# Filler matmuls on zeros spread over the first stages of an attention and expert kernel on one core

## The chip, the cores and the metric

The kernel runs on one core of a Trainium2 chip. Its time is device microseconds (us) of one execution, and kernels are compared by the median of their runs. TensorE (PE) multiplies, VectorE (DVE), ScalarE (ACT) and GpSimd (POOL) work element by element, and SyncE (SP) issues transfers. [...]

## What is computed

Two stages, cut from the reference to what matters:

```python
# q, k, v: (2, 8, 576, 64)
q_d, k_d, v_d = (t.reshape(B, H, 144, 4, D).mean(axis=3) for t in (q, k, v))
out_d = softmax(scale * q_d @ k_d.T) @ v_d               # pooled attention
out_up = np.repeat(out_d, 4, axis=2)
mask = np.abs(pos[:, None] - pos[None, :]) < 4           # a narrow band
out_local = softmax(np.where(mask, scale * q @ k.T, -1e9)) @ v
attn_out = out_up + out_local
x = attn_out.transpose(0, 2, 1, 3).reshape(1152, 512)
p = domain_probs / (domain_probs.sum(-1, keepdims=True) + 1e-9)
for e in range(4):                                       # w1: (4, 512, 1024), w2: (4, 1024, 512)
    out += p[:, e:e + 1] * (np.maximum(x @ w1[e], 0) @ w2[e])
```

## The kernel before

The attention is done in four parts, a0 to a3: two batches, each in two halves of 288 positions. The names of steps and tiles follow from that.

- Keys and queries come in with positions on the partitions and are transposed by PE through the identity: k00t, k01t (batch 0, halves 0 and 1), k10t, k11t for keys and a0.qt for queries, each in four steps (`transposed`, L309). A copy (k01te, a0.qte) brings each result out of PSUM.
- Pooled keys and queries are sums over four positions, k01ds and a0.qds on DVE or GpSimd (L342, L343), transposed by k01dt and a0.qdt (`pooled_rows`, L348).
- Pooled attention runs in four groups of two heads. In group 0 of a0: a0.ds0 scores (`dscores`, L628), a0.dm0 and a0.dn0 maxima, a0.de0 exponentials, a0.da0, a0.db0 and a0.dq0 normalisation, a0.dt0 transposes (`dtrans`, L680), a0.dv0 values (`dvalues`, L697).
- Local attention runs in three tiles of queries: a0.sc1.0 and a0.sc1.1 are two halves of the scores of tile 1 (`scores`, L485; for a0 a matmul with the mask goes ahead, L475), then max, sub, exp, sum and norm, block transposes on DVE (a0.blk) and a0.pv1 the values (`values`, L565).
- a0.xs, a0.xh and a0.xl add both attentions and split the sum into xhi and xlo, the experts' input in two parts.

The experts follow. Expert 0 takes the tokens in four chunks, m00 to m03, and forms its products in three terms each from halves of the weights (whi, wlo) and of x. m00.m0 to m00.m7 are the first products of chunk 0 (`m1`, L730: twelve matmuls of 128x256, into a tile m00h each). ACT's m00.r0 takes the positive part (`relu`, L737), and DVE's m00.l0 takes the rest (`rest`, L741); m00h has been read then. m00.o00 and on are the second products (L755). The other chunks and experts 1 to 3 come after 90 us and fill the rest of the span.

The order of all this is written out by hand. Each piece of work is a named step, `steps` holds them, and `ORDER` (L22) is the list in which the loop at L1043 runs them; what a step issues is put at the end of its engine's instructions. Waits come from the data: an instruction waits until what it reads is written, and until the buffer that it writes into is free. The buffers matter here. PSUM tiles come from three pools (L145 to L147): ps_s, ps_g with three buffers, ps_m with three buffers. A tile takes the next buffer of its pool in turn, and the buffer passes on only when the last instruction that uses its former tile is done. ps_m serves two tiles of scores of a0 (a0sb), all m00h tiles, the second products, and the tile of the fillers:

```python
WARM = [14, 0, 0, 0, 0, 0, 0, 0, 0, 0, 0, 0, 0, 1, ...]      # L21
wz = big.tile([P, 64], F32, name="wz")                        # L177
def warm(i, n):
    if "wps" not in T:
        T["wps"] = ps_m.tile([P, 512], F32, tag="m", name="wps")
    for _ in range(n):
        nc.tensor.matmul(T["wps"][:64, :64], wz, wz, start=True, stop=True)
for i, n in enumerate(WARM):
    step(f"warm{i}", "P", [], lambda i=i, n=n: warm(i, n))
```

A filler is one matmul of zeros with zeros, whose result nobody reads. `WARM` says how many each of the 40 steps warm0 to warm39 issues: 31 in all, 22 of them ahead of PE's first real step a0.qdt. The last ones stand ahead of a0.dv1.

Of the kernel before, what the change touches and what calls it, by code (L numbers as in the profile page):

```python
# [21 lines left out]
ORDER = """  # L22
    q0n.0 q0n.1 k00n.0 k00n.1 a0.qds.0 kstart0 q0r.0 k00r.0 q0r.1 a0.qds.1 k00ds.1 k00r.1 warm15 warm36 warm33 warm5
    warm6 warm21 warm37 warm20 warm0 warm22 warm13 warm18 a0.qdt k00t.0 warm10 k00t.1 warm29 a0.qt.0 a0.qt.2 warm34
    warm2 a0.qt.3 a0.qt.1 warm16 k01n.0 v00n.1 v00n.0 k01n.1 v01n.1 warm23 raw100 v01n.0 a1q.1 a1q.2 a1q.0 a1q.3
    vw01 raw101 k00ds.0 a0.qde k01ds.1 v00d.0 a0.start v01d.1 v00d.1 v01d.0 k00te.1 k00te.0 a0.qte.0 warm4 k00t.2
    warm19 a0.qte.2 a0.qte.1 k00t.3 k00te.3 k00te.2 a0.qte.3 a0.sc0.0 a0.sc0.1 warm12 warm25 warm31 warm14 warm30
    k00dt vw00 k01r.1 k01ds.0 warm24 k01dt a0.sc1.0 a0.sc1.1 warm17 k01de k00de k01r.0 a0.max0 a0.sub0 k01t.1 warm11
    k01t.0 a0.max1 k01te.1 a0.sub1 a0.ds1 warm3 a0.ds0 k01t.2 a0.dm1 a0.dn1 k01te.0 a0.exp0 warm39 a0.sc2.0 a0.ds2
    warm7 k01t.3 warm1 a0.exp1 a0.dm0 a0.de1 a0.dn0 a0.sum1 a0.de0 a0.da1 k01te.2 a0.da0 a0.db0 a0.sum0 a0.db1  # L30
    a0.ds3 a0.dm2 a0.dn2 a0.dm3 k01te.3 warm9 a0.sc2.1 warm35 warm38 a0.dq0 a0.dt0 a0.dc0 a0.eps0 a0.dq1 a0.dn3
    a0.rec0 a0.max2 a0.de2 a0.sub2 warm28 warm27 a0.dt1 a0.norm0 a0.da2 a0.dc1 a0.db2 a0.dq2 a0.de3 a0.da3 a0.eps1
    a0.db3 a0.blk0.1 a0.rec1 a0.exp2 a0.blk0.0 a0.sum2 a0.dq3 a0.norm1 whi100.1 wlo100.1 a0.eps2 a0.blk1.1 a0.rec2
    a0.blk1.0 warm26 a0.dv1 a0.dt2 a0.dc2 a0.norm2 whi101.0 a0.dv0 a0.dt3 a0.dv2 warm8 a0.dc3 a0.pv0 a0.dv3 a1.qt.1
    whi100.0 a0.xd a0.xs0 a1.qt.3 a0.pv1 a1.qt.2 a0.blk2.0 a0.blk2.1 vw02 k10r.3 raw200 k10r.2 praw raw201 k10r.1
    a0.xh0 a0.xs1 a0.xl0 wlo100.0 a1.start a1.qte.1 a1.qte.3 wlo101.0 a1.qte.2 a0.pv2 a0.xs2 a0.xh2 a1.qt.0 whi200.1
    whi101.1 wlo101.1 whi200.0 a1.qte.0 a0.xh1 a0.xl2 a1.qd.1 a0.xl1 a1.qd.0 a1.sc1.1 a1.sc2.1 a1.sc2.0 warm32
    a1.sc0.1 m00.m0 a1.ds0 a1.ds1 m00.m3 a1.dm0 a1.dn0 a1.de0 a1.madd2 a1.dm1 a1.da0 wlo200.1 a1.dn1 a1.sc0.0 a1.ds2
    wlo200.0 m00.r0 m00.l0 a1.madd0 whi201.1 a1.de1 whi201.0 m00.r3 a1.db0 a1.dq0 a1.da1 a1.max2 a1.dm2 m00.m2
    a1.sc1.0 a1.dt0 a1.db1 a1.dn2 a1.madd1 a1.dc0 a1.de2 a1.da2 a1.ds3 kstart1 a1.dq1 m00.m1 m00.r2 m00.r1 a1.max0  # L40
    m00.l3 a1.dm3 a1.dn3 a1.db2 wlo201.1 m00.l1 a1.sub0 a1.dq2 a1.sub2 a1.dt1 m00.m6 a1.de3 a1.dc1 m00.m4 m00.r4
    a1.exp0 a1.exp2 k11r.3 vw03 k11r.0 k10r.0 v11n.1 vw05 vw04 v10n.1 k11r.1 k11r.2 a1.da3 a1.dv1 a1.db3 a1.max1
    a1.dq3 m00.l2 a1.dt2 k10t.2 a1.dv0 m00.o00 a1.dt3 a1.dc2 a1.dc3 m00.r6 k10te.2 a1.sum2 a1.sum0 m00.l4 wlo201.0
    a1.eps0 a1.sub1 m00.m5 a1.dv3 k10t.0 a1.dv2 k10t.1 m00.o01 m00.m7 a1.eps2 gate a1.rec2 a1.rec0 a1.norm0 m00.l6
    a1.blk0.0 a1.norm2 a1.exp1 k10te.0 m00.r5 m00.l5 a1.sum1 a1.eps1 k10te.1 a1.xd a1.blk0.1 k11t.1 a1.pv0 k11te.1
    a1.rec1 a1.norm1 m00.r7 a1.xs0 a1.blk2.1 m00.l7 a1.blk2.0 a1.blk1.1 k10t.3 k11t.0 m00.o10 m00.o02 k11t.3 k11t.2
    k11te.0 k10te.3 a1.blk1.0 a1.pv2 k11te.3 k11te.2 k11d.1 a1.pv1 a1.xs1 a1.xh1 a1.xl1 a1.xs2 a1.xh2 a1.xh0
    a2.start a1.xl0 a1.xl2 k10d.0 k10d.1 m00.o11 m00.o03 m00.g0 a2q.3 a2q.2 a2q.1 a2q.0 m00.o12 a2.qt.2 a2.qt.0
    a2.qt.1 m01.m0 a2.qte.1 a2.qte.0 m01.r0 a2.qd.0 k11d.0 m01.m1 v11d.1 a2.qte.2 a2.qt.3 a2.qte.3 a2.qd.1 a2.ds0
    m00.o13 a2.sc0.1 a2.sc0.0 m00.g1 m01.l0 a2.ds2 m01.m3 a2.dm2 a2.dn2 v11n.0 v10n.0 a2.de2 a2.madd0 a2.dm0 a2.dn0  # L50
    a2.de0 a2.da0 a2.da2 a2.max0 a2.db0 m01.r3 m01.r1 a2.dq0 v10d.1 v10d.0 a2.ds1 m01.m2 m01.r2 a2.db2 m01.l1 a2.dq2
    m01.l2 a2.dm1 a2.dn1 a2.sc2.1 a2.sc2.0 a2.sc1.0 a2.dt0 a2.sc1.1 a2.ds3 a2.dt2 a2.dc0 a2.madd1 a2.de1 a2.da1
    a2.max1 m01.l3 a2.madd2 a2.sub1 vw12 a3q.2 v11d.0 vw10 a3q.1 a3q.3 vw11 a3q.0 m01.m6 m01.m4 m01.r4 a2.dc2
    a2.max2 a2.db1 a2.exp1 m01.l4 a2.dm3 a2.dn3 a2.sub2 a2.exp2 a2.de3 m01.m5 m01.r5 m01.o10 a3.qt.1 a2.sum1 a2.dq1
    a2.da3 m01.l5 m01.r6 a2.db3 a3.start a2.dv0 a2.dt1 a2.dv2 m01.o00 m01.m7 a2.dq3 a2.dc1 a2.dt3 m01.o11 m01.l6
    a2.sub0 a2.exp0 a2.dc3 a2.sum0 a2.eps1 a2.rec1 a2.norm1 a2.eps0 a3.qte.1 a2.rec0 a2.norm0 a2.blk1.0 m01.o12
    a2.dv1 a3.qt.0 a3.qt.2 m01.o01 a2.dv3 m01.r7 a2.sum2 a2.blk0.0 a2.eps2 a2.rec2 a2.blk1.1 a2.norm2 a3.qte.2 a2.xd
    a3.qte.0 a2.blk0.1 a2.pv0 a2.blk2.1 a2.blk2.0 a2.pv1 a3.qt.3 m01.o02 vw14 vw13 vw15 a2.pv2 a3.qte.3 a3.sc1.0
    m01.l7 a3.qd.0 a2.xs1 a2.xh1 a2.xs0 a2.xh0 a3.qd.1 a2.xl0 a2.xl1 a3.ds0 m01.o13 m01.o03 a3.sc1.1 a3.sc0.1 m01.g0
# [1011 lines left out]
```

## Time and profile before

| | |
|---|---|
| median of three runs | 482.71 us |
| the runs | 481.98, 482.71, 1521.41 us |
| the profiled execution's own time | 481.98 us |
| its span in the trace | 480.2 us |
| busy: PE, DVE, ACT, POOL | 466.3, 277.8, 162.7, 54.7 us |

The span runs from the first to the last instruction of the profiled execution; 1.8 us of its own time lie around it. One of the three runs is far off the two others, and the median leaves it aside. [...] A busy engine is one that has an instruction under way, at whatever clock.

### The profile page before, as it was taken

Reading aid. Unit: us, or ns where it says so; the run is one execution under the profiler, and the core shown is the slowest. Engines: PE = TensorE matmul, PEld = TensorE weight load, DVE = VectorE, ACT = ScalarE, POOL = GpSimd, SP = SyncE. Lnnn points to the kernel's source line nnn. Section 1 sums busy time; section 2 is a strip of 40 time slices with the busy share of each in tenths; the row PEclk is TensorE's granted clock in tenths of the full one; section 3 lists DMA queues with packets and bytes.
Section 4 is the critical chain, followed back from the end, with each engine's and each line's share of the span. In section 5 each row is a group of like instructions: output and inputs, shape, how many; then the busy total and the mean of one; then the engine's idle time right before and its main releaser. Section 6 shows DMA issues by size and latency. Waiting matters only on the chain.

```text
span 480.2 us, 8723 instructions
## 1 busy us (share of the span) xinstructions
PE 466.3 (97%) x3710; PEld 414.9 (86%) x3710; DVE 277.8 (58%) x493; ACT 162.7 (34%) x277; POOL 54.7 (11%) x68
## 2 busy tenths in 40 slices
...
PEclk8555979999999999999999999999999999999999
...
GB/s 177 210 227 140 60 66 74 129 69 0 68 3 5 41 46 44 89 87 71 105 44 0 1 27 62 46 87 89 44 1 0 60 30 45 45 0 45 44 67 44
DMA packets 49574, 29.90 MB, mean 62 GB/s; under 512 B 26816, under 2 KB 43392, under 8 KB 49536
## 3 DMA queue, kind: packets, MB, share of 16 engines
...
q8 instruction: 29, 0.48, 0.4%
q14 instruction: 9, 0.07, 0.0%
HBM read 26.99 MB, written 2.36 MB: 61 GB/s over the span
## 4 chain that ended last, share of the span: by engine, by line
PE 89%; DVE 5%; DMA 3%; SPq 1%; issue 1%; ACT 1%; ACTq 0%
PE X L936 16%; PE Z L936 8%; PE Y L936 4%; PE m03h L730 3%; PE m03o L755 3%; DMA k01n<-in_k_dram 2%; PE m02h L730 2%; PE m01o L755 2%; PE m01h L730 2%; PE m02o L755 2%; PE m00o L755 2%; PE m00h L730 2%; DVE ptb L556 1%; PE o L993 1%; PE o28None L993 1%; PE o18None L993 1%
## 5 line engine op out<-in xcount | busy, mean ns | idle before, releaser
L975 ACT ACTIVATE hh<-H 128x1024 fp32r<-128x1024 f32 (+1 forms) x30 | 28.9, 974 | 92.1 <-PE o10None L993 4.9
L978 DVE SCALAR_TENSOR_TENSOR ho<-H,hh 128x1024 fp32r<-128x1024 f32 (+1 forms) x30 | 33.6, 1119 | 24.5 <-ACT hh L975 24.5
L888 DVE TENSOR_TENSOR wo<-r,wh 128x1792 fp32r<-128x1792 f32 x12 | 24.3, 2023 | 22.8 <-PE Z L936 18.9
L945 ACT ACTIVATE H<-X 128x576 f32<-128x576 f32 x24 | 15.6, 650 | 55.5 <-PE X L936 55.5
L936 PE MATMUL X<-xc,wh 128*128 128x288 f32 x192 | 33.2, 295 | 0.0
L936 PEld LDWEIGHTS X<-xc,wh 128*128 128x128 f32 x192 | 28.2, 188 | 0.0
L936 PE MATMUL X<-xhi,wo 128*128 128x288 f32 x96 | 20.7, 296 | 0.0
L936 PE MATMUL X<-xlo,wh 128*128 128x288 f32 x96 | 20.6, 296 | 0.0
L936 PE MATMUL X<-xhi,wh 128*128 128x288 f32 x96 | 20.6, 295 | 0.0
L936 PE MATMUL X<-xc,wo 128*128 128x288 f32 x96 | 20.5, 295 | 0.0
L170 ACT CAST wh<-r 128x1792 fp32r<-128x1792 f32 x12 | 20.3, 1689 | 0.3 <-DVE r L880 0.3
L170 ACT CAST v<-q 128x1024 fp32r<-128x1024 f32 x12 | 12.2, 1044 | 15.7 <-PE o18None L993 7.2
L274 POOL TENSOR_TENSOR wlo<-raw,whi 128x1024 fp32r<-128x1024 f32 x7 | 16.7, 2392 | 5.2 <-ACT whi L170 5.1
L949 DVE TENSOR_TENSOR H<-H,Z 128x576 f32<-128x576 f32 x12 | 9.0, 749 | 14.2 <-PE Z L936 14.2
L936 PE MATMUL Z<-xc,wh 128*128 128x288 f32 x96 | 16.6, 294 | 0.0
L936 PEld LDWEIGHTS X<-xhi,wo 128*128 128x128 f32 x96 | 15.6, 188 | 0.2
L936 PEld LDWEIGHTS X<-xlo,wh 128*128 128x128 f32 x96 | 15.4, 188 | 0.0
L936 PEld LDWEIGHTS X<-xhi,wh 128*128 128x128 f32 x96 | 15.4, 188 | 0.0
L936 PEld LDWEIGHTS X<-xc,wo 128*128 128x128 f32 x96 | 15.3, 188 | 0.0
L949 DVE TENSOR_TENSOR H<-H,Y 128x576 f32<-128x576 f32 x12 | 9.0, 749 | 10.8 <-PE Y L936 6.6
L911 DVE TENSOR_TENSOR v<-q,v 128x1024 fp32r<-128x1024 f32 x12 | 14.6, 1219 | 0.9 <-ACT v L170 0.9
L755 PE MATMUL m03o<-whi,m03t 128*128 128x512 f32 x48 | 15.0, 390 | 0.0
...
## 6 DMA issues: line engine op xcount, KB each, us to landing
...
```

What stands on the lines that cost most here:

```text
L170: nc.scalar.copy(out_, in_)
L274: engine(f"wlo{nm}.{i}").tensor_tensor(dst, T["raw" + nm][:, sl], T["whi" + nm][:, sl], ALU.subtract)
L730: nc.tensor.matmul(ps[:, :n], w[:, d, cc:cc + P], x[:, d, n0:n0 + n], start=i == 0, stop=i == len(terms) - 1,)
L755: nc.tensor.matmul(ps[:, cs], T[f"{nm}t{f}"][:, hpart, cc:cc + P], w[:, f % 4, cs], start=f == 0 and x == 0, stop=f == KF - 1 and x == 2,)
L888: engine(f"wo{e}{i}").tensor_tensor(w, T[f"r{e}{i}"], f32(T[f"wh{e}{i}"]), ALU.subtract)
L911: engine(f"vo{e}{q}").tensor_tensor(w[:, 1], T[f"q{e}{q}"], f32(w[:, 0]), ALU.subtract)
L936: nc.tensor.matmul(ps[:, n, :NH // 2], w[:, d * P:(d + 1) * P], x[:, d, n * (NH // 2):(n + 1) * (NH // 2)], start=u == 0 and first_, stop= ...
L945: nc.scalar.mul(dst, at("Z" if c == "t22" else "X"), -1.0)
L949: nc.vector.tensor_tensor(dst, dst, at({"h11": "Y", "h12": "Z", "h22": "X"}[c]), ALU.add)
L975: nc.scalar.activation(htile("hh", t, u), hrows(t, u), AF.Relu)
L978: nc.vector.scalar_tensor_tensor(htile("ho", t, u), hrows(t, u), 0.0, f32(htile("hh", t, u)), ALU.max, ALU.subtract)
L993: nc.tensor.matmul(T[o][:, cs], T[f"{hpart}{e}{t}"][:, f % 4 * 2 + f // 4], T[f"v{e}{q}"][:, w, f % 2 * 512 + cs.start:f % 2 * 512 + cs.stop],
```

## The change

`WARM` gets 42 more entries, 179 fillers in all, and `ORDER` gets the steps warm40 to warm81, each directly in front of a step of PE. Nothing else changes; lines below the two tables move down by three (L206 becomes L209, L730 becomes L733).

```diff
-WARM = [14, 0, 0, ..., 2, 0, 1, 3, 0, 0]
+WARM = [14, 0, 0, ..., 2, 0, 1, 3, 0, 0, 26, 8, 11, 3, 3, 3, 3, 3, 3, 4, 6, 2, 4, 3, 3, 3, ..., 3, 3, 3, 10, 4, 8]
...
-    warm6 warm21 warm37 warm20 warm0 warm22 warm13 warm18 a0.qdt k00t.0 warm10 k00t.1 warm29 a0.qt.0 a0.qt.2 warm34
+    warm6 warm21 warm37 warm20 warm0 warm22 warm13 warm18 warm40 a0.qdt warm41 k00t.0 warm10 k00t.1 warm29 warm42
```

| new steps | fillers | where |
|---|---|---|
| warm40, 41, 42 | 26, 8, 11 | ahead of a0.qdt, k00t.0, a0.qt.0 |
| warm43 to 50 | 28 | from a0.qt.2 to k01dt |
| warm51 to 62 | 36 | from a0.sc1.0 to a0.sc2.1 |
| warm63 to 74 | 36 | from a0.dt0 to a0.pv1 |
| warm75 to 78 | 12 | from a1.qt.2 to a1.sc1.1 |
| warm79, 80, 81 | 10, 4, 8 | ahead of a1.sc1.0 (just behind m00.m2), a1.dt0, m00.m6 |

PE's instructions at its start, before. wps is the fillers' tile, wz the zeros, a_qdt the pooled queries, k00t the keys and a_qt the queries of a0; xN counts equal instructions in a row.

```order
L206 MATMUL wps<-wz 64x64 x22
L348 MATMUL a_qdt<-ident,a0.qdp 128x72 x4
L309 MATMUL k00t_183<-ident,acc 128x72 x4
L309 MATMUL k00t_188<-ident,acc 128x72 x4
L309 MATMUL a_qt_193<-ident,acc 128x72 x4
L309 MATMUL a_qt_198<-ident,acc 128x72 x4
L206 MATMUL wps<-wz 64x64 x2
L309 MATMUL a_qt_205<-ident,acc 128x72 x4
```

And now:

```order
L209 MATMUL wps<-wz 64x64 x48
L351 MATMUL a_qdt<-ident,a0.qdp 128x72 x4
L209 MATMUL wps<-wz 64x64 x8
L312 MATMUL k00t_217<-ident,acc 128x72 x4
L312 MATMUL k00t_222<-ident,acc 128x72 x4
L209 MATMUL wps<-wz 64x64 x11
L312 MATMUL a_qt_238<-ident,acc 128x72 x4
L209 MATMUL wps<-wz 64x64 x3
L312 MATMUL a_qt_246<-ident,acc 128x72 x4
L209 MATMUL wps<-wz 64x64 x5
L312 MATMUL a_qt_256<-ident,acc 128x72 x4
```

The real steps keep their order; 26 fillers more stand ahead of the first, and groups of 8, 11, 3 and 3 between the next ones.

The same engine from the transposes of the second half's keys (k01t) to the last scores of a0 (a0sl), before. a0sd are the pooled scores.

```order
L309 MATMUL k01t_382<-ident,kr_322 128x72 x4
L628 MATMUL a0sd_394<-kd_141,a0qd 72x144 x2
L628 MATMUL a0sd_397<-kd_141,a0qd 72x144 x2
L309 MATMUL k01t_400<-ident,kr_322 128x72 x4
L475 MATMUL a0sl<-mask,ident 128x128 x2
L485 MATMUL a0sl<-kT_140,a0qT 32x32 x16
```

And now:

```order
L312 MATMUL k01t_467<-ident,kr_389 128x72 x4
L209 MATMUL wps<-wz 64x64 x3
L631 MATMUL a0sd_482<-kd_141,a0qd 72x144 x2
L209 MATMUL wps<-wz 64x64 x3
L631 MATMUL a0sd_488<-kd_141,a0qd 72x144 x2
L209 MATMUL wps<-wz 64x64 x3
L312 MATMUL k01t_494<-ident,kr_389 128x72 x4
L209 MATMUL wps<-wz 64x64 x3
L478 MATMUL a0sl<-mask,ident 128x128 x2
L488 MATMUL a0sl<-kT_140,a0qT 32x32 x16
```

Three fillers stand between any two steps, and the two pairs of pooled scores no longer follow each other directly.

PE among the experts' first products, with the engine whose semaphore an instruction waits for in brackets, before. The first m00h is m00.m2, a1sl are scores of a1, a1pdt the transposes of a1.dt0, a1sd pooled scores, and the last m00h is m00.m1.

```order
L730 MATMUL m00h_823<-xhi,wlo_533 128x256 x4
L730 MATMUL m00h_823<-xhi,whi_531 128x256 x4
L730 MATMUL m00h_823<-xlo,whi_531 128x256 x4
L485 MATMUL a1sl<-kT_140,a1qT 32x32 [waits DVE_49]
L485 MATMUL a1sl<-kT_140,a1qT 32x32 x15
L680 MATMUL a1pdt_852<-ident,a1pd_774 72x72 [waits Pool_49]
L680 MATMUL a1pdt_852<-ident,a1pd_774 72x72 x3
L628 MATMUL a1sd_867<-kd_141,a1qd 72x144 [waits Activation_49]
L628 MATMUL a1sd_867<-kd_141,a1qd 72x144
L730 MATMUL m00h_875<-xhi,wlo_533 128x256 x4
```

And now:

```order
L733 MATMUL m00h_980<-xhi,wlo_648 128x256 [waits DVE_49]
L733 MATMUL m00h_980<-xhi,wlo_648 128x256 x3
L733 MATMUL m00h_980<-xhi,whi_646 128x256 x4
L733 MATMUL m00h_980<-xlo,whi_646 128x256 x4
L209 MATMUL wps<-wz 64x64 x10
L488 MATMUL a1sl<-kT_140,a1qT 32x32 [waits DVE_49]
L488 MATMUL a1sl<-kT_140,a1qT 32x32 x15
L209 MATMUL wps<-wz 64x64 x4
L683 MATMUL a1pdt_1023<-ident,a1pd_931 72x72 [waits Pool_49]
L683 MATMUL a1pdt_1023<-ident,a1pd_931 72x72 x3
L631 MATMUL a1sd_1038<-kd_141,a1qd 72x144 [waits Activation_49]
L733 MATMUL m00h_1046<-xhi,wlo_648 128x256 [waits DVE_49]
```

Both products now begin with a wait for DVE: for m00.m2 it is the instruction of m00.l0, for m00.m1 that of m00.l3. The tile wps is in use until the eight fillers ahead of m00.m6, which come later still.

## Rows read from the trace of the kernel before

**Rows 1.** The page: busy time of each engine (with its share of the span and its instructions), and the clock granted to PE in forty slices of the span, in tenths of full speed.

```profile
PE 466.3 (97%) x3710; PEld 414.9 (86%) x3710; DVE 277.8 (58%) x493; ACT 162.7 (34%) x277; POOL 54.7 (11%) x68
...
PEclk8555979999999999999999999999999999999999
```

**Rows 2.** Stretches of the span. Columns: start and end in us, length, then busy us (and instructions) of PE, PE's weight loads, DVE, ACT and POOL, the granted clock as a share of full speed, the DMA engines' busy share, and GB/s.

```profile
4.20:7.61 3.41, 1.35 (x19) 1.07 (x17) 3.26 (x9) 1.04 (x1) 2.13 (x4) 1.00 0.80 194
7.61:19.62 12.01, 8.99 (x112) 7.30 (x112) 5.95 (x10) 7.63 (x11) 5.91 (x7) 0.50 0.91 229
19.62:48.57 28.95, 27.80 (x425) 23.01 (x425) 21.08 (x61) 14.87 (x38) 16.36 (x16) 0.50 0.70 180
35.31:42.57 7.26, 7.04 (x59) 6.02 (x57) 7.01 (x15) 3.62 (x7) 6.70 (x6) 0.50 0.90 264
48.57:58.81 10.24, 8.66 (x132) 7.37 (x128) 8.52 (x21) 6.70 (x19) 6.45 (x7) 1.00 0.28 62
58.81:65.64 6.83, 6.01 (x31) 5.74 (x30) 5.31 (x12) 1.73 (x7) 5.83 (x6) 0.50 0.02 4
65.64:90.00 24.36, 23.38 (x211) 20.09 (x211) 16.45 (x42) 8.32 (x20) 4.28 (x6) 1.00 0.53 114
90.00:480.00 390.00, 386.94 (x2766) 347.14 (x2765) 214.19 (x328) 121.12 (x184) 12.28 (x16) 1.00 0.15 44
```

**Rows 3.** PE's timeline in the first 5.3 us. Columns here and in all timelines below: start in us, duration in us, engine, line, operation, tile written and tiles read, shape, count, and in brackets the idle time just before and what ended it.

```profile
0.98 3.25 PE L206 MATMUL wps<-wz 128*64 128x64 f32 x28 [0.98 <-DVE wz L178]
...
4.02 1.19 PE L206 MATMUL wps<-wz 128*64 128x64 f32 x16
```

**Rows 4.** All instructions of the tile wps: count, shortest, median and longest duration in ns, and the first and last start in us.

```profile
L206 PE MATMUL wps<-wz x62: 222/314/369, 1.0 to 33.8; 128*64 128x64 f32 x62
```

**Rows 5.** PE's timeline up to 20.4 us: the steps ahead of which it waited.

```profile
6.49 0.34 PE L348 MATMUL a_qdt<-ident,a0.qdp 72*128 72x72 f32 x2 [1.29 <-POOL kT L377]
8.18 0.50 PE L348 MATMUL a_qdt<-ident,a0.qdp 72*128 72x72 f32 x2 [1.34 <-DVE a0.qdp L343]
...
11.78 1.22 PE L309 MATMUL a_qt<-ident,acc 72*128 72x72 f32 x8 [1.23 <-DVE a0qd L172]
...
19.67 0.74 PE L348 MATMUL k01dt<-ident,k01dp 72*128 72x72 f32 x4 [0.46 <-DVE k01dp L343]
```

**Rows 6.** PE's timeline between 24 and 44 us: one row for each kind of step.

```profile
24.17 1.58 PE L628 MATMUL a0sd<-kd,a0qd 64*72 64x144 f32 x8
...
26.22 1.15 PE L475 MATMUL a0sl<-mask,ident 128*128 128x128 f32 x4
27.30 0.47 PE L485 MATMUL a0sl<-kT,a0qT 64*32 64x32 f32 x32
27.70 1.23 PE L628 MATMUL a0sd<-kd,a0qd 64*72 64x144 f32 x4
28.86 0.74 PE L309 MATMUL k01t<-ident,kr 72*128 72x72 f32 x4
...
42.57 1.55 PE L565 MATMUL a0pv<-ptb,vw 128*64 128x96 f32 x16 [0.22 <-DVE a0x L578]
```

**Rows 7.** PE's timeline between 52 and 78 us: steps of the same kinds.

```profile
52.45 0.35 PE L485 MATMUL a1sl<-kT,a1qT 64*32 64x32 f32 x32
52.73 0.71 PE L628 MATMUL a1sd<-kd,a1qd 64*72 64x144 f32 x4
...
72.26 0.47 PE L309 MATMUL k10t<-ident,acc 72*128 72x72 f32 x4
...
76.80 0.88 PE L565 MATMUL a1pv<-ptb,vw 128*64 128x96 f32 x16
```

**Rows 8.** PE's timeline among the experts' first products and just behind them.

```profile
53.37 0.73 PE L730 MATMUL m00h<-xhi,wlo 128*128 128x256 f32 x4
...
56.07 0.36 PE L485 MATMUL a1sl<-kT,a1qT 64*32 64x32 f32 x32 [1.04 <-DVE a1pm L508]
56.98 0.45 PE L680 MATMUL a1pdt<-ident,a1pd 72*72 72x72 f32 x4 [0.55 <-POOL a1pd L672]
...
57.99 0.74 PE L730 MATMUL m00h<-xhi,wlo 128*128 128x256 f32 x4
...
61.57 1.22 PE L730 MATMUL m00h<-xhi,wlo 128*128 128x256 f32 x4 [0.82 <-DVE m00t L741]
...
66.41 0.71 PE L697 MATMUL a1po<-a1pts,vd 72*64 72x72 f32 x8
```

**Rows 9.** DVE's timeline in the same stretch.

```profile
55.28 0.41 DVE L741 SCALAR_TENSOR_TENSOR m00t<-m00h,m00t 128x256 fp32r<-128x256 f32 x1
...
58.81 2.05 DVE L665 TENSOR_SCALAR a1dsm<-a1dsm 72x2 f32<-72x2 f32 x1 [0.29 <-ACT a1pd L655]
...
61.10 0.41 DVE L741 SCALAR_TENSOR_TENSOR m00t<-m00h,m00t 128x256 fp32r<-128x256 f32 x1
```

**Rows 10.** POOL's timeline there.

```profile
58.47 2.36 POOL L274 TENSOR_TENSOR wlo<-raw,whi 128x1024 fp32r<-128x1024 f32 x1
```

**Rows 11.** Three more stretches, columns as in rows 2.

```profile
35.00:38.00 3.00, 3.00 (x22) 2.33 (x21) 2.85 (x10) 2.17 (x4) 2.21 (x4) 0.50 1.09 305
45.60:48.50 2.90, 2.90 (x142) 2.42 (x138) 2.08 (x5) 1.59 (x3) 0.00 (x0) 0.50 0.15 34
55.40:58.80 3.40, 2.18 (x46) 1.79 (x47) 2.87 (x10) 2.90 (x11) 1.71 (x5) 1.00 0.00 0
```

More of the change, by code (lines that the diff above doesn't have):

```diff
@@ L22 @@
+WARM = [14, 0, 0, 0, 0, 0, 0, 0, 0, 0, 0, 0, 0, 1, 0, 0, 1, 0, 0, 0, 0, 3, 0, 0, 0, 0, 1, 3, 2, 0, 0, 0, 0, 0, 2, 0, 1, 3, 0, 0, 26, 8, 11, 3, 3, 3, 3, 3, 3, 4, 6, 2, 4, 3, 3, 3, 3, 3, 3, 3, 3, 3, 3, 3, 3, 3, 3, 3, 3, 3, 3, 3, 3, 3, 3, 3, 3, 3, 3, 10, 4, 8]
 ORDER = """
     q0n.0 q0n.1 k00n.0 k00n.1 a0.qds.0 kstart0 q0r.0 k00r.0 q0r.1 a0.qds.1 k00ds.1 k00r.1 warm15 warm36 warm33 warm5
-    warm6 warm21 warm37 warm20 warm0 warm22 warm13 warm18 a0.qdt k00t.0 warm10 k00t.1 warm29 a0.qt.0 a0.qt.2 warm34
@@ L25 @@
[L25 to L59, printed above, removed]
+    warm6 warm21 warm37 warm20 warm0 warm22 warm13 warm18 warm40 a0.qdt warm41 k00t.0 warm10 k00t.1 warm29 warm42
@@ new lines @@
+    a0.qt.0 warm43 a0.qt.2 warm34 warm2 warm44 a0.qt.3 warm45 a0.qt.1 warm16 k01n.0 v00n.1 v00n.0 k01n.1 v01n.1
+    warm23 raw100 v01n.0 a1q.1 a1q.2 a1q.0 a1q.3 vw01 raw101 k00ds.0 a0.qde k01ds.1 v00d.0 a0.start v01d.1 v00d.1
+    v01d.0 k00te.1 k00te.0 a0.qte.0 warm4 warm46 k00t.2 warm19 a0.qte.2 a0.qte.1 warm47 k00t.3 k00te.3 k00te.2
+    a0.qte.3 warm48 a0.sc0.0 a0.sc0.1 warm12 warm25 warm31 warm14 warm30 warm49 k00dt vw00 k01r.1 k01ds.0 warm24
+    warm50 k01dt warm51 a0.sc1.0 warm52 a0.sc1.1 warm17 k01de k00de k01r.0 a0.max0 a0.sub0 warm53 k01t.1 warm11
@@ new lines @@
+    warm54 k01t.0 a0.max1 k01te.1 a0.sub1 warm55 a0.ds1 warm3 warm56 a0.ds0 warm57 k01t.2 a0.dm1 a0.dn1 k01te.0
+    a0.exp0 warm39 warm58 a0.sc2.0 warm59 a0.ds2 warm7 warm60 k01t.3 warm1 a0.exp1 a0.dm0 a0.de1 a0.dn0 a0.sum1
+    a0.de0 a0.da1 k01te.2 a0.da0 a0.db0 a0.sum0 a0.db1 warm61 a0.ds3 a0.dm2 a0.dn2 a0.dm3 k01te.3 warm9 warm62
+    a0.sc2.1 warm35 warm38 a0.dq0 warm63 a0.dt0 a0.dc0 a0.eps0 a0.dq1 a0.dn3 a0.rec0 a0.max2 a0.de2 a0.sub2 warm28
+    warm27 warm64 a0.dt1 a0.norm0 a0.da2 a0.dc1 a0.db2 a0.dq2 a0.de3 a0.da3 a0.eps1 a0.db3 a0.blk0.1 a0.rec1 a0.exp2
```

29 lines of the change are left out of this document (28 added, 1 removed).

## The prediction

> **What bounds the kernel now.** I read the page first. TensorE (PE) is busy for 97% of the span, and one line of the page spoils that picture: the granted clock of PE is low near the start [rows 1]. The table of stretches says where: PE is granted half its clock (1.2 GHz) from 7.61 to 48.57 us and again from 58.81 to 65.64 us, and the full 2.4 GHz otherwise [rows 2]. After 90 us PE is busy for 386.94 of 390.00 us, so what is won or lost before that reaches the end of the kernel undiminished. The question is only when PE gets through the first 66 us.
>
> In the slow stretch PE looks full: 27.80 of 28.95 us from 19.62 to 48.57 [rows 2]. But this is busy at half speed, and other things set times there too. Before 19.67 PE waits for others four times, last for VectorE (DVE), which sums the keys of k01n [rows 5]. That ends at 19.62 whatever PE does, since it hangs on a transfer. From 35.31 to 42.57 DVE is busy for 7.01 of 7.26 us [rows 2], and the second step of pooled values (a0.pv1) starts at 42.57 when DVE lets go of a buffer [rows 6].
>
> **The price of a filler.** The 31 fillers of before leave 62 records, two per matmul [rows 4]. At 1.2 GHz 28 records take 3.25 us, less the last one's tail of 0.31: 0.109 us apart, so 0.21 us per filler. The later 16 records take 1.19 us, less 0.22: 0.065 us apart, with the first two gaps still at the old pace 0.058, so 0.12 us per filler at 2.4 GHz [rows 3, 4]. All 179 new ones are then 21 us of PE time at the full clock and 38 us at half of it. What counts is where they lie.
>
> **The change, leg by leg**, at the full clock, against the profiled execution (481.98 us, of which 480.2 are the span; the median of the runs shown is 482.71).
>
> 1. Up to 19.67 us: 73 fillers. The first 45 (26, 8, 11) stand where PE idled 1.29, 1.34 and 1.23 us and a little more [rows 5]; 45 x 0.12 = 5.4 us about fills that. PE thus has no pause in which the level fell before, which is after 4.20 to 7.61 us with 1.35 us of work in 3.41 [rows 2]. The other 28 cost 3.4 us, and PE's own 8.99 us of work in 7.61 to 19.62 halves. The leg ends with DVE: 0 us.
>
> 2. 19.67 to 31.08 (to the last scores of a0). Per step, half clock against full clock, each with its tail: four transposes 0.74 against 0.47, pooled scores (ds) 1.23 against 0.71, 16 score matmuls 0.47 against 0.35 [rows 6, 7]. Two mask matmuls cost 1.15 and have no row at the full clock: between 0.58 (all halves) and 1.15 I take 0.6, as the other long steps nearly halve. Savings: five transposes 1.35, two ds 1.04, the pair of ds, which now no longer run together, 1.58 - 2 x 0.71 = 0.16, two masks 1.1, four scores 0.48: 4.1 us. In the same leg stand 36 new fillers, in front of steps that PE would start at once: 36 x 0.12 = 4.3 us. Net 0. The fillers eat the clock's gain.
>
> 3. 31.08 to 42.57: 36 fillers, 4.3 us, beside PE's real work of some 11 us that falls to 6. That is 10.3 of 11.5 us, and DVE's chain covers it [rows 2]: 0. If that cover is gone, it costs up to 1 us.
>
> 4. 42.57 to 48.57: two steps of pooled values fall from 1.55 to 0.88, two transposes by 0.27 each, four blocks of scores by 0.12 each [rows 6, 7]: 2.4 us saved, against twelve fillers, 1.4 us. Net -1.0, so the experts' first product (m00.m0) starts near 47.6 in place of 48.6.
>
> 5. Its neighbours, 48.57 to 66.41. Here the change adds more than the 22 fillers. The three PSUM buffers of ps_m are shared by the fillers' tile wps and the tiles m00h. Before, wps is free after the last filler ahead of a0.dv1; now its last filler stands ahead of m00.m6, so m00h has two buffers instead of three. The order with its waits shows it: m00.m2 now waits for DVE, and m00.m1 too, where neither did. What they wait for is the reading of m00h two steps earlier (m00.l0 and m00.l3). Before, m00.m2 started at 53.37 [rows 8], and m00.l0 ran from 55.28 to 55.69, behind DVE's other work [rows 9]. So m00.m2 starts 2.3 us later, at 55.7 on before's scale. It takes 1.66 (53.37 to 55.03, as 56.07 less its idle 1.04 [rows 8]), and the ten fillers that were to fill that idle time now come behind it: 1.2 us. Then scores 0.3, four fillers 0.5, transposes 0.4, ds 0.65: 60.4. DVE's next steps read these, yet DVE has slack there: its 2.05 us instruction at 58.81 [rows 9] is a tiny one that lasts as long as GpSimd's wlo from 58.47 to 60.83 [rows 10]. So m00.l3 still ends near 61.5, and only then m00.m1 starts (before: 57.99). m00.m1 1.6, transposes 0.4, eight fillers 0.9, then m00.m6 and m00.m4 at the full clock 3.3: 67.7 in place of 66.41. That is +1.3 with the full clock throughout.
>    The level will not hold throughout, I think. In 55.40 to 58.80 of before, PE worked 2.18 of 3.40 us and the level fell at its end [rows 11]; the new wait leaves PE idle for 2.3 us in one piece. Bounds for this: nothing, or a stretch as long as 58.81 to 65.64 that costs half of PE's work in it, 3 us. I take +1.1, nearer the short end, as ten fillers follow at once. Leg: +2.4.
>
> Sum: 481.98 + 0 + 0 + 0 - 1.0 + 2.4 = **483.4 us**. That is 0.1% over the median of the runs, while about 2% (9.7 us) is what a measurement of this kernel can tell from no change.
>
> **What speaks against the full clock.** From 35.00 to 38.00 us PE is busy 3.00 of 3.00 us, the level stays at 0.50, and much of this work is transposes and narrow products; from 45.60 to 48.50 it is as busy, with score matmuls, and the level rises at its end [rows 11]. So being busy is not enough; what runs matters. [...]
>
> **Rivals.**
> - *The level falls back early, and the fillers run at half clock* (slower). Place: 14 to 48 us, where three fillers stand between steps of transposes. Price: 112 new fillers from 11.78 us to m00.m0 at 0.21 us are 23.5 us, less the idle time that takes them up, 1.15 us after 19.62 [rows 2] and about 0.9 before it: +21.5, with leg 5's +1.3 about 504 us. It decides (over 492.4) once half clock lasts for more than about half of that stretch. For it: rows 11. [...] Likeliest time if it decides: 496; a shorter fall gives 486 to 492.
> - *The fillers are hidden after all* (faster). If the steps of legs 2 and 4 wait for ScalarE and DVE anyhow, the fillers cost nothing there: 4.1 + 2.4 = 6.5 us saved, at most. With leg 5's +1.3 that is 477; without any cost of the lost buffer, and with the second slow stretch gone (4.84 us from 61.57 to 66.41 [rows 8] becoming 3.3), 474. Against it: PE is busy 27.80 of 28.95 us there, so little of it waits.
> - *The lost buffer costs nothing* (no change): m00.m2 waits less since DVE comes earlier. Then -1.0 and -1.5: 479.5.
>
> **How the numbers follow.** My forecast and what lies close (479.5 to 486): 0.55. Fillers hidden or buffer free (474 to 479.5, a little below): 0.15, of which 0.05 lie under 473.1. A shorter fall (486 to 492.4): 0.17. A long fall (over 492.4): 0.13. So faster 0.05, same 0.82, slower 0.13. The range 475 to 493 leaves out about 0.07 below and 0.12 above. The price of the filler bounds it from both sides: free on the low side, 0.21 us each for half of the stretch on the high side.
>
> **What would show it.** Right: granted clock 1.00 from 4.2 us to beyond 48 us; m00.m0 starting 0.5 to 2 us earlier than 48.6; PE idle about 2 us just ahead of m00.m2, released by DVE's m00t; a fresh dip of the clock in 52 to 66. Leg 2 fails if sc2.1 ends well before 31; leg 5 fails if m00.m2 starts without a wait, or if a1.dv1 starts before 65. The whole fails if the row of the granted clock shows 0.50 over most of 14 to 48 us.

## The result, and the profile after

The changed kernel takes 489.19 us (median of four runs, 487.21 to 490.02) against 482.35 us for the kernel before: a ratio of 1.0137, with a 95% interval from 1.0107 to 1.0168. That is 1.4% slower, inside 2% and inside the predicted range of 475 to 493 us, and 5.8 us above the forecast of 483.4. The forecast was 1.4 us more than the profiled execution before; the medians lie 6.8 us apart. The profiled execution took 487.21 us, of which 485.4 are the span.

The page of the changed kernel, the two lines that answer to [rows 1]:

```profile
PE 474.8 (98%) x4068; PEld 424.3 (87%) x4068; DVE 278.8 (57%) x493; ACT 163.1 (34%) x277; POOL 54.3 (11%) x68
...
PEclk9999999999999999999999999999999999999999
```

TensorE has 358 more records (two per filler), and the row of the clock reads full in every slice. At the very start it is not: the trace has no record of the clock before it first rises, and such a stretch reads 1.00. The fillers' own pace tells where it rose, in two pieces of TensorE's timeline:

```profile
1.79 4.47 PE L209 MATMUL wps<-wz 128*64 128x64 f32 x40
...
6.27 2.94 PE L209 MATMUL wps<-wz 128*64 128x64 f32 x47
```

The 40 records are 0.107 us apart (4.47 less the last one's 0.31, over 39), the pace of half clock in [rows 3]; the 47 are 0.059 apart, the pace of full clock. So the clock rose near 6.3 us, before at 4.20 [rows 2], and from there on it is full (1.00 from 6.27 to 480 us). The change does what its fillers can do for the clock, and the kernel is slower all the same. Where the time went is read leg by leg. Stretches of the changed kernel, cut at the same steps as in [rows 2] (columns as there):

```profile
4.20:19.62 15.42, 15.42 (x236) 14.02 (x235) 8.73 (x17) 7.83 (x11) 7.47 (x10) 1.00 0.88 225
22.03:34.90 12.87, 12.87 (x246) 10.51 (x244) 5.08 (x21) 4.91 (x15) 4.62 (x7) 1.00 0.80 214
34.90:46.19 11.29, 10.59 (x173) 9.34 (x156) 9.35 (x26) 6.19 (x17) 7.98 (x8) 1.00 0.59 172
46.19:51.36 5.17, 5.17 (x193) 4.77 (x193) 4.79 (x11) 4.07 (x7) 1.71 (x1) 1.00 0.09 21
51.36:71.64 20.28, 15.75 (x212) 13.98 (x205) 14.61 (x32) 8.26 (x25) 13.24 (x12) 1.00 0.15 34
```

TensorE is busy for all of 15.42 and of 12.87 us in the first two rows, at the full clock from 6.3 us on. It has become the bound there, by fillers. The starts of the steps that end the legs:

| leg | before, us | after, us | difference | predicted |
|---|---|---|---|---|
| 1, to k01dt | 19.67 | 22.03 | +2.4 | 0 |
| 2, to the last scores of a0 | 11.41 | 12.87 | +1.5 | 0 |
| 3, to a0.pv1 | 11.49 | 11.29 | -0.2 | 0 |
| 4, to m00.m0 | 6.00 | 5.17 | -0.8 | -1.0 |
| 5, to a1.dv1 | 17.84 | 20.28 | +2.4 | +2.4 |
| the rest of the span | 413.79 | 413.76 | 0.0 | 0 |

The sum is +5.2 us, the difference of the two profiled executions (487.21 less 481.98). The three other executions were 1.3 to 2.8 us longer, with mean granted clocks of 0.996 and 0.993 against 0.999: somewhere in them the clock did dip, and only the profiled one has a trace.

Leg 1 in TensorE's timeline, for [rows 3, 5] (columns as there):

```profile
0.98 8.22 PE L209 MATMUL wps<-wz 128*64 128x64 f32 x96 [0.98 <-DVE wz L181]
9.13 0.62 PE L351 MATMUL a_qdt<-ident,a0.qdp 72*128 72x72 f32 x4
9.69 1.15 PE L209 MATMUL wps<-wz 128*64 128x64 f32 x16
10.76 0.73 PE L312 MATMUL k00t<-ident,acc 72*128 72x72 f32 x8
11.42 1.50 PE L209 MATMUL wps<-wz 128*64 128x64 f32 x22
12.85 0.47 PE L312 MATMUL a_qt<-ident,acc 72*128 72x72 f32 x4
...
22.03 0.47 PE L351 MATMUL k01dt<-ident,k01dp 72*128 72x72 f32 x4
```

The waits of before are gone. The fillers ahead of a_qdt end at 9.13, where before the second half of that step stood at 8.18. The queries start at 12.85 (before 11.78), and from there to k01dt it takes 9.18 us, before 7.89. The late rise of the clock has a small part in this: in a kernel with the same instructions up to here (the first experiment below) the pace changes at about 4.0 us, the queries start at 12.51 and k01dt at 21.70. No row of this stretch has an idle time: k01dt no longer waits for DVE, it waits for its turn.

Legs 2 and 5 in the same timeline:

```profile
25.12 0.47 PE L312 MATMUL k01t<-ident,kr 72*128 72x72 f32 x4
25.52 0.56 PE L209 MATMUL wps<-wz 128*64 128x64 f32 x6
26.01 0.47 PE L312 MATMUL k01t<-ident,kr 72*128 72x72 f32 x4
...
51.36 0.74 PE L733 MATMUL m00h<-xhi,wlo 128*128 128x256 f32 x4
...
58.43 0.74 PE L733 MATMUL m00h<-xhi,wlo 128*128 128x256 f32 x4 [2.12 <-DVE m00t L744]
...
60.03 1.38 PE L209 MATMUL wps<-wz 128*64 128x64 f32 x20
61.34 0.35 PE L488 MATMUL a1sl<-kT,a1qT 64*32 64x32 f32 x32
...
65.71 0.74 PE L733 MATMUL m00h<-xhi,wlo 128*128 128x256 f32 x4 [2.39 <-DVE m00t L744]
...
71.64 0.71 PE L700 MATMUL a1po<-a1pts,vd 72*64 72x72 f32 x8
```

A group of three fillers fills the time from 25.52 to 26.01: 0.49 us, 0.16 per filler, against 0.12 in a long row. Its neighbours grow too. Four transposes and their group take 0.89 us (25.12 to 26.01). Four transposes up to the fillers take 0.40 (25.12 to 25.52), eight of k00t in a row 0.66 (10.76 to 11.42), so four more in a row cost 0.26. So the group costs 0.63 us between two transposes. In leg 5 the two new waits are there, both released by DVE's reading of m00h, and the ten fillers come behind the first of them.

DVE and GpSimd in the same stretch, for [rows 9, 10]:

```profile
57.97 0.41 DVE L744 SCALAR_TENSOR_TENSOR m00t<-m00h,m00t 128x256 fp32r<-128x256 f32 x1
...
63.63 1.37 DVE L668 TENSOR_SCALAR a1dsm<-a1dsm 72x2 f32<-72x2 f32 x1 [0.46 <-ACT a1pd L658]
...
65.25 0.41 DVE L744 SCALAR_TENSOR_TENSOR m00t<-m00h,m00t 128x256 fp32r<-128x256 f32 x1
```

```profile
61.90 0.11 POOL L379 MEMSET kT<- 128x16 f32 x1 [2.29 <-PE a1sl L488]
...
62.64 2.34 POOL L277 TENSOR_TENSOR wlo<-raw,whi 128x1024 fp32r<-128x1024 f32 x1
```

The second reading, m00.l3, starts 13.89 us after m00.m0 (65.25 less 51.36); before it was 12.53 (61.10 less 48.57). The small instruction ahead of it (L668) has ACT's values at 63.63 and lasts until 65.00, when GpSimd's wlo ends (64.98), as it did before (60.86 and 60.83). And wlo comes later: it starts 11.28 us after m00.m0, before 9.90 (58.47 less 48.57), because GpSimd waits for scores (a1sl) that stand behind m00.m2 and the ten fillers. So the first wait delays the reading that ends the second. ACT's values come later too (12.27 us after m00.m0, before 10.24); what each of the two would have cost alone is not shown.

### The profile page after: what moved, and what is told of

Same layout as the page of the kernel before. It is cut to its first block, busy times and chain, and to the rows that moved or that the text cites. A ratio compares the mean times of both kernels' runs of the same rounds, so it can differ in the third digit from the quotient of the medians.

```text
span 485.4 us, 9439 instructions
## 1 busy us (share of the span) xinstructions
PE 474.8 (98%) x4068; PEld 424.3 (87%) x4068; DVE 278.8 (57%) x493; ACT 163.1 (34%) x277; POOL 54.3 (11%) x68
## 4 chain that ended last, share of the span: by engine, by line
PE 94%; DVE 4%; ACT 1%; issue 1%; ACTq 0%
PE X L939 16%; PE Z L939 8%; PE wps L209 5%; PE Y L939 4%; PE m03h L733 3%; PE m03o L758 3%; PE m02h L733 2%; PE m01h L733 2%; PE m01o L758 2%; PE m02o L758 2%; PE m00h L733 2%; PE m00o L758 2%; DVE ptb L559 1%; PE o L996 1%; PE o28None L996 1%; PE o18None L996 1%
## 5 line engine op out<-in xcount | busy, mean ns | idle before, releaser
L209 PE MATMUL wps<-wz 128*64 128x64 f32 x420 | 35.5, 237 | 1.0 <-DVE wz L181 1.0
L209 PEld LDWEIGHTS wps<-wz 128*64 128x64 f32 x420 | 30.1, 148 | 4.0 <-DVE wz L181 1.0
```

## Experiments

### The three late groups left out

```diff
-WARM = [..., 3, 10, 4, 8]
+WARM = [..., 3, 0, 0, 0]
```

> The changed kernel without its last three groups of fillers (10, 4, 8 ahead of a1.sc1.0, a1.dt0 and m00.m6), so that the tile wps is done before m00.m0 and m00h has three buffers again. Theory (two late waits for DVE, 2.12 and 2.39 us, are the price of the lost buffer): both waits go, a1.dv1 starts 2 to 4 us sooner after m00.m0 than the 20.3 us of the changed kernel, time about 486 us. Rival (the fillers there hold the clock, the buffer is cheap): granted clock falls to half in 55 to 69 us as in the kernel before, and the stage keeps 20 us or more; time 489 us or above.

Measured: 486.71 us, ratio 1.0104 (1.0073 to 1.0135). Both new waits, ahead of m00.m2 and of m00.m1, are gone from the trace, and leg 5 takes 15.90 us (51.02 to 66.92) in place of 20.28. Less came through than that, because of a wait that is new, later on, and because the clock fell right behind it. TensorE's timeline and a stretch of this kernel:

```profile
79.28 0.99 PE L312 MATMUL k11t<-ident,acc 72*128 72x72 f32 x3 [2.10 <-DMA acc<-in_k_dram]
```

```profile
79.08:85.91 6.83, 6.52 (x35) 5.28 (x36) 5.22 (x12) 0.68 (x1) 0.00 (x0) 0.50 0.00 0
```

The transposes of the next keys (k11t) waited for their transfer. From a1.dv1 to the end it took 418.1 us in place of 413.8.

### The buffer held, with one filler and nothing else

```diff
-WARM = [14, ..., 3, 0, 0, 26, 8, 11, 3, ..., 10, 4, 8]
+WARM = [14, ..., 3, 0, 0, 0, 0, 0, 0, ..., 0, 0, 1]
```

> The kernel before with one single filler added, ahead of m00.m6, so that wps is in use until there and m00h has two buffers. Nothing else is added. Theory (the lost buffer alone costs the stage its two waits): slower than before by 1.3 to 3 us, about 484 to 485.5 us. Rival (it costs nothing by itself, only with the fillers): 482.4 us as before.

Measured: 484.65 us, ratio 1.0056 (1.0038 to 1.0073): by the ratio 2.7 us for one single filler. TensorE's timeline shows the price at the two places:

```profile
54.86 0.74 PE L733 MATMUL m00h<-xhi,wlo 128*128 128x256 f32 x4 [2.35 <-DVE m00t L744]
...
61.66 1.22 PE L733 MATMUL m00h<-xhi,wlo 128*128 128x256 f32 x4 [2.18 <-DVE m00t L744]
```

The lost buffer alone makes both waits, at the lower clock of the kernel before as well. Leg 5 takes 21.25 us (47.38 to 68.63) in place of 17.84. The changed kernel's leg 5, at the full clock, lost 2.4.

### The early groups only

```diff
-WARM = [..., 26, 8, 11, 3, 3, 3, ..., 10, 4, 8]
+WARM = [..., 26, 8, 11, 0, 0, 0, ..., 0, 0, 0]
```

> The changed kernel with only its first three groups of new fillers (26, 8, 11); the groups from a0.qt.2 on are left out, and wps is free as early as before. Theory A (the later groups are needed to hold the clock): half clock from about 14 to 48 us, time 482.4 plus about 1 us for the first group that overshoots, 483.5 us. Theory B (real work holds a level that has once risen): full clock throughout to 48 us, legs 2 and 4 keep their savings of 4.1 and 2.4 us, time 477 us.

Measured: 482.20 us, ratio 1.0022 (0.9997 to 1.0047): no difference clear of the noise. The granted clock:

```profile
4.19:17.84 13.65, 11.85 (x217) 10.59 (x215) 6.70 (x14) 8.13 (x12) 6.73 (x9) 1.00 0.91 204
17.84:51.98 34.14, 32.02 (x464) 26.88 (x458) 24.93 (x67) 17.24 (x40) 20.72 (x19) 0.50 0.71 182
```

Theory A holds: without the later groups the clock fell at 17.84 us, though TensorE was busy for 32 of the next 34 us. The early groups alone gain and cost nothing that can be told from the noise.

### One filler in place of three

```diff
-WARM = [..., 26, 8, 11, 3, 3, 3, 3, 3, 3, 4, 6, 2, 4, 3, ..., 3, 10, 4, 8]
+WARM = [..., 26, 8, 11, 1, 1, 1, 1, 1, 1, 1, 1, 1, 1, 1, ..., 1, 10, 4, 8]
```

> The changed kernel with every group of warm43 to warm78 cut to one filler. Theory (in the changed kernel's trace a group of three costs 0.50 to 0.56 us, of which only 0.06 us per record is the work and the rest the change from one kind of step to another and back): a group of one costs about 0.3 us, so 24 groups in legs 1, 2 and 4 save 0.23 us each plus the groups that were longer: 5 to 6 us, time about 483.5 us, if the clock holds. Rival (the clock needs the triples): half clock over part of 14 to 48 us, time 487 us or above.

Measured: 494.56 us, ratio 1.0247 (1.0207 to 1.0288). The rival holds:

```profile
4.85:21.91 17.06, 15.56 (x250) 13.30 (x253) 7.70 (x12) 9.75 (x14) 7.92 (x11) 1.00 0.90 199
21.91:56.05 34.14, 34.12 (x431) 27.69 (x434) 20.35 (x60) 14.23 (x36) 16.20 (x16) 0.50 0.58 150
```

Fewer fillers were slower by 5 us: the clock fell at 21.91 us, and the fillers that were left ran at half of it, on top of all the real work. That is the prediction's first rival (slower, by fillers at half clock), which gave 496 us. The changed kernel is on the good side of it by its count of fillers.

### Fillers of 128 columns

```diff
-    wz = big.tile([P, 64], F32, name="wz")
+    wz = big.tile([P, P], F32, name="wz")
...
-            nc.tensor.matmul(T["wps"][:64, :64], wz, wz, start=True, stop=True)
+            nc.tensor.matmul(T["wps"][:, :64], wz, wz[:, :64], start=True, stop=True)
```

> The changed kernel with all fillers made 128 columns wide (the zeros are loaded as 128x128 weights in place of 128x64); their number, place and tile stay. In the changed kernel's trace a filler record is 0.058 us behind another one, but 0.155 us lie between a transpose (72 rows by 128 columns) and a filler (128 by 64), and 0.15 back. Theory (the price is the change of the array's division into columns, not the filler): beside transposes and other steps of 128 columns both pauses go, a group of three between two transposes costs 0.36 in place of 0.56 us, elsewhere one of two pauses goes; 24 groups in legs 1, 2 and 4 save 0.1 to 0.2 us each, 2.5 to 4.5 us: 485 to 486.7 us. Rival (the pause comes with any change of step, by its waits): the pauses stay, 489 us.

Measured: 555.06 us, ratio 1.1513 (1.1469 to 1.1557). Neither theory foresaw it. Two more kernels have the same filler:

> Fillers 128 columns wide, one in place of three or more in warm43 to warm78, 18 in place of 26 ahead of a0.qdt, none in warm79 to warm81 (so m00h has its three buffers). Theory (wide fillers keep the clock up with less of them): full clock to 48 us, legs 1, 2 and 4 cost 7 us less than in the changed kernel, the buffer gives 2.5 us: 479 to 480 us, faster than both kernels. Rival (single fillers don't hold the clock, wide or not, as with the narrow ones, where it fell at 21.9 us): half clock over part of 22 to 56 us, 485 to 492 us.

> Fillers 128 columns wide, 18 in place of 26 ahead of a0.qdt, none in warm79 to warm81, all others as in the changed kernel. Theory: the clock is held to 48 us and beyond as in the changed kernel, 2.5 us come back by the buffer, 1 us by the shorter first group, 2.5 to 4.5 us by the pauses between divisions of the array: 481.5 to 483.5 us. Rival (pauses stay): 485.5 us.

They took 514.69 and 546.29 us (ratios 1.0673, 1.0647 to 1.0699, and 1.1326, 1.1303 to 1.1350), outside all that was expected of them, and tell the same. TensorE's timeline in the first of the three, and a stretch of it:

```profile
31.11 0.69 PE L312 MATMUL a_qt<-ident,acc 72*128 72x72 f32 x4
31.59 1.47 PE L209 MATMUL wps<-wz 128*128 128x64 f32 x6
32.85 0.69 PE L312 MATMUL a_qt<-ident,acc 72*128 72x72 f32 x4
...
115.75 1.22 PE L733 MATMUL m00h<-xhi,wlo 128*128 128x256 f32 x4
...
119.19 0.74 PE L733 MATMUL m00h<-xhi,wlo 128*128 128x256 f32 x4
```

```profile
20.00:60.00 40.00, 40.00 (x329) 39.12 (x329) 6.29 (x14) 8.28 (x15) 5.26 (x6) 1.00 0.50 134
```

Three things are to be seen. First, a wide record takes 0.21 us (1.26 us from 31.59 to 32.85 for six) where a narrow one took 0.107 at half clock. Second, TensorE ran at half clock up to 118 us: the same product takes 1.22 us at 115.75 and 0.74 at 119.19. The column of the clock says 1.00 for the stretch from 20 to 60 us all the same, as it does ahead of 6.3 us in the changed kernel: there is no record of the clock before it first rises, here at about 118 us by these rows. And TensorE was busy for 40.00 of 40.00 us there. Third, the theory on the pauses is borne out in the one place where it can be seen: four transposes between wide fillers take 0.48 us (31.11 to 31.59), 0.12 each and no pause, while in the kernel before, at half clock too, eight transposes that start at 11.78 [rows 5] and the change to narrow fillers took 1.15 us, 0.96 of it at 0.12 each. The next row of the kernel before shows where the fillers begin:

```profile
12.93 0.69 PE L206 MATMUL wps<-wz 128*64 128x64 f32 x4
```

So a change from steps of 128 columns to fillers of 64 takes about 0.2 us at half clock (1.15 less 0.96) and, in the changed kernel, 0.155 us between a transpose and a narrow filler where records of one kind are 0.06 apart. What it was worth in a whole kernel stayed hidden behind the price of the wide filler. Why wide fillers kept the clock at half is open.

### The late groups in another tile

```diff
+        o = T["a1sl"][:64, 0, 448:] if i >= 79 else T["wps"][:64, :64]
         for _ in range(n):
-            nc.tensor.matmul(T["wps"][:64, :64], wz, wz, start=True, stop=True)
+            nc.tensor.matmul(o, wz, wz, start=True, stop=True)
```

> The changed kernel with the fillers of warm79 to warm81 written to columns of the scores' tile a1sl that nothing else uses, so that wps is done before m00.m0 and m00h has three buffers, with all 210 fillers kept. Theory (the buffer, not the fillers, costs leg 5 its time): the waits of 2.12 and 2.39 us ahead of m00.m2 and m00.m1 go, and the time is that of the kernel without the three groups or up to 1.5 us above it, 486.5 to 488 us. Rival (the 22 fillers cost by themselves): 489 us or more.

Measured: 485.60 us, ratio 1.0071 (1.0046 to 1.0096), 3.6 us under the changed kernel with the same number of fillers. Leg 5 takes 16.59 us (52.20 to 68.79). So the buffer is what cost leg 5 its time. The 22 fillers cost 0.7 us of the leg (against 15.90). They may bring it back, for the profiled execution has a mean granted clock of 1.000, against 0.993 without them, and the median is 1.1 us below that of the kernel without them, but the two intervals overlap: this is not shown.

### Fillers that stream 128 columns

```diff
-    wz = big.tile([P, 64], F32, name="wz")
+    wz = big.tile([P, P], F32, name="wz")
...
+        o = T["a1sl"][:64, 0, 384:] if i >= 79 else T["wps"][:64, :P]
         for _ in range(n):
-            nc.tensor.matmul(T["wps"][:64, :64], wz, wz, start=True, stop=True)
+            nc.tensor.matmul(o, wz[:, :64], wz, start=True, stop=True)
```

with 18 fillers ahead of a0.qdt, and one (then two) in each of warm43 to warm78.

> Built on the kernel with the last three groups in a1sl (485.6 us). Every filler now streams 128 columns of zeros through its 64 columns of weights in place of 64; warm43 to warm78 have one filler each, a0.qdt has 18 in front of it in place of 26. From the run with 128 weight columns (0.213 us a record at half clock against 0.107 with 64, at the same 64 streamed columns) a record's price is that of its weight load, so the longer stream should cost nothing more: 0.107 and 0.058 us a record. Theory A (a longer stream makes a filler count for more with the clock, and ones suffice): full clock to 48 us and beyond, legs 1, 2 and 4 save 24 x 0.23 us and 1 us at the start: 479 to 480 us, below both kernels. Theory B (one filler in a group doesn't hold the clock, whatever it streams): half clock for a long part of 20 to 56 us, 486 us or above.  Theory C (the longer stream doubles a record's price): 484 us or above with the full clock.

> As the kernel before it in this job, with two fillers of 128 streamed columns in each of warm43 to warm78. Theory A (price by the weight load, and the clock held): 24 x 0.12 us and 1 us saved against 485.6: 481.5 to 482.5 us, the time of the kernel before. Theory B (the clock is not held by pairs): 486 us or above. Theory C (price by the stream): 485 us.

Measured: 489.69 us (ratio 1.0175, 1.0124 to 1.0225) and 493.11 us (1.0233, 1.0190 to 1.0276). Theory C is right on the price. TensorE's timeline of the first:

```profile
12.04 1.96 PE L210 MATMUL wps<-wz 128*64 128x128 f32 x16
13.93 0.72 PE L313 MATMUL k00t<-ident,acc 72*128 72x72 f32 x8
...
19.50 0.43 PE L210 MATMUL wps<-wz 128*64 128x128 f32 x2
19.86 0.47 PE L313 MATMUL a_qt<-ident,acc 72*128 72x72 f32 x4
```

Sixteen records take 1.89 us, 0.118 each with the two pauses, where narrow ones took 1.07 (9.69 to 10.76 above). The long early groups alone put the first queries at 17.13 us in place of 12.85. Theory A is right on the clock: with one long filler (0.36 us) between two steps, four transposes of keys or queries took 0.47 us each time from 17.13 to 45.46 us, the pace of the full clock [rows 7], and 0.74 only at 49.28; with one narrow filler the clock had fallen at 21.91. With two the profiled execution has a mean granted clock of 1.000, and the time is 3.4 us longer.

### A mixture, and the next wait behind it

The mixture takes narrow fillers for the early groups, long ones between the steps, the late groups in a1sl:

```diff
-    wz = big.tile([P, 64], F32, name="wz")
+    wz = big.tile([P, P], F32, name="wz")
...
+        w = P if 43 <= i <= 78 else 64
+        o = T["a1sl"][:64, 0, 448:] if i >= 79 else T["wps"][:64, :w]
         for _ in range(n):
-            nc.tensor.matmul(T["wps"][:64, :64], wz, wz, start=True, stop=True)
+            nc.tensor.matmul(o, wz[:, :64], wz[:, :w], start=True, stop=True)
```

and the last kernel also moves two transfers:

```diff
-    k11r.3 vw03 k11r.0 k10r.0 v11n.1 vw05 vw04 v10n.1 k11r.1 k11r.2 a1.da3 ...
+    k11r.3 vw03 k11r.0 k10r.0 k11r.1 k11r.2 v11n.1 vw05 vw04 v10n.1 a1.da3 ...
```

> A mixture of what the runs so far gave: fillers ahead of a0.qdt, k00t.0 and a0.qt.0 narrow (64 streamed columns; 18, 8, 11), warm43 to warm78 one filler each of 128 streamed columns (four ahead of a0.pv1, where PE waits for DVE), warm79 to warm81 narrow and in a1sl. From the run with such singles: 11.68 us from k01dt to a0.dt0 and 11.18 to a0.pv1, full clock but for one dip. Theory: k01dt at 20 to 20.5 us, m00.m0 at 48 to 48.6, a1.dv1 near 65. From there theory A (the gain is kept): 480.5 us, about 1.5 us below the kernel before. Theory B (the second half's keys of batch 1, k11t, wait for a transfer that SyncE issues only behind one that waits for GpSimd's wlo, as the runs with an early a1.dv1 showed, with 0.8 to 2.1 us of waiting): 482 us, no gain.

> As the mixture, with the two transfers k11r.1 and k11r.2 issued ahead of v11n.1, which waits for GpSimd's wlo, in place of behind it and ten more transfers. Theory B: the wait of PE ahead of k11t for its transfer goes, and 0.5 to 2 us are gained over the mixture: 480.5 us. Theory A (nothing waited there): as the mixture.

Measured: 483.76 us (ratio 1.0054, 1.0033 to 1.0075) and 482.62 us (1.0011, 0.9991 to 1.0031). In the mixture TensorE waits for the keys' transfer:

```profile
77.77 0.28 PE L314 MATMUL k11t<-ident,acc 72*128 72x72 f32 x1 [1.16 <-DMA acc<-in_k_dram]
78.42 0.35 PE L314 MATMUL k11t<-ident,acc 72*128 72x72 f32 x2 [0.37 <-DMA acc<-in_k_dram]
```

With the two transfers moved the same step is one row without a wait:

```profile
76.17 0.42 PE L314 MATMUL k11t<-ident,acc 72*128 72x72 f32 x4
```

Theory B holds for the place, and the move is worth 1.1 us by the medians; the two intervals do not overlap. The hoped-for 480.5 us did not come: a1.dv1 started at 66.34 and 66.13 us, as in the kernel before (66.41), not near 65. No kernel of this study beats the kernel before.

## Why the prediction was right, and where it was not

**The time and the mechanism.** The time lies inside the range, but above the 479.5 to 486 us that had most of the chance. It lies where the prediction put a shorter fall of the clock (486 to 492.4), and no such fall is in the profiled execution: fillers that cost more than their price brought it there. That the range held is in this respect luck.

**What bounds the kernel.** That the first 66 us decide was right: the rest of the span is the same to 0.03 us.

**The price of a filler** was the term that was mis-sized. It was read from long rows of fillers, 0.12 us each, and applied to groups of three between other steps, where the rows above show 0.49 to 0.63 us a group, 0.16 to 0.21 each, in place of 0.36. In leg 2 the twelve groups (22.43 to 34.62) take 5.9 us by their rows in place of 4.3. The other side of that leg was right: without them it takes 12.87 - 5.9 = 7.0 us against 11.41, so 4.4 us saved, 4.1 predicted. The leg's +1.5 is this one error: 5.9 less 4.4. In the prediction 1.2 and 2.4 GHz stand for the granted shares 0.50 and 1.00 [rows 2]. The trace gives the shares alone. As a pace, in the kernel before, four records of m00h with 256 columns take 0.85 us at 0.50 (62.59 to 63.44), 1.2 columns a ns, and 0.47 at 1.00 (49.13 to 49.60), 2.2. At a column a clock the first would be 1.2 GHz, an estimate, and 2.4 its double.

**Leg 1** had the cover wrong. The prediction let it end with DVE at 19.67. The groups from the first queries to k01dt take 4.8 us by their rows (31 fillers, 3.7 predicted), and the queries began 1.07 us late behind the longer first groups, about 0.3 of it by the late rise of the clock. Both together put TensorE past DVE. (TensorE's waits before 19.67 were six, not four; the two that the prediction leaves out are 0.65 and 0.17 us.)

**Legs 3 and 4** came out as predicted: DVE covers leg 3, and leg 4 gains 0.8.

**Leg 5** has the predicted sum, and half of it for another reason. The lost buffer, the two waits and DVE as their releaser were right, and so was the first delay: m00.m2 starts 7.07 us after m00.m0, 4.80 before, 2.3 predicted and 2.27 measured. Two steps were wrong. DVE was said to have slack for the second wait, measured against GpSimd's wlo, which was taken to end at 60.83 as before. But wlo stands behind scores that the first wait moves: it started 11.28 us after m00.m0 in place of 9.90, and m00.m1 came 14.35 us after m00.m0, where the prediction's 61.5 means 12.9. The experiments agree as far as DVE shows it: its small instruction ahead of m00.l3, which ended with wlo in the kernels before and after (60.86 and 60.83, 65.00 and 64.98), ended 13.58 us after m00.m0 with the buffer held and nothing else (59.27 + 1.69, less 47.38), 12.20 and 12.41 in the two kernels that free it, against 13.64 in the changed kernel and 12.29 before. And the clock, for which 1.1 us had been put in, did not fall in the profiled execution. One error made up for the other there. The kernel with the buffer held and nothing else shows that the buffer is the cause.

**The rivals.** The first is real, but belongs to kernels with fewer fillers: with ones it gave 494.56 us. That fillers are hidden is refuted for legs 1 and 2, where TensorE is busy without a gap, and holds for leg 3. That the buffer costs nothing is refuted by three runs, one that holds it and two that free it.

**The signs that were named.** Clock full beyond 48 us: right, but from about 6.3 us, not from 4.2. m00.m0 0.5 to 2 us earlier: wrong, 2.8 us later. About 2 us of idle time ahead of m00.m2: right, 2.12. A fresh dip of the clock in 52 to 66: not in the profiled execution.

Open is how much the full clock would be worth without fillers: no kernel here held it for nothing. The mixture came closest, with 11.68 us from k01dt to a0.dt0, against 11.41 before, so there too fillers took back what the clock gave. Of the 50 executions of the kernel before that were timed beside the experiments, seven have a mean granted clock of 0.993 to 1.000, and they took no less than the others (medians 481.9 and 481.8 us). Either the full clock gained nothing there, or it did not rise before some 48 us, which would read as 1.00; none of the seven has a trace.
